# Moving the ordered expert list and one gather ahead of a product, loading gate weights earlier, and packing two weight chunks per buffer slot

## Chip, cores and metric

The kernel runs on one core of one Trainium2 chip. The metric is device time in microseconds (us) of one execution of the program. The inputs are fixed, so every run does the same work.

## What is computed

Three layers follow each other. The first is attention over 4 batches, 12 heads, 448 positions and 64 values a head, in which the heads are mixed by one small matrix before the softmax and by another behind it. The second is a dense layer with an ELU between two matrices. The third sends each of the 1792 rows to one of 8 experts, or to none:

```python
h = x @ w_in                                   # 1792x768 @ 768x2048
x = np.where(h > 0.0, h, np.exp(np.minimum(h, 0.0)) - 1.0) @ w_out
do_compute = x @ w_skip > 0                    # rows that go to an expert at all
logits = x[do_compute] @ w_gate                # 8 logits a row
e_idx = np.argmax(logits, axis=1)
gate_w = softmax(logits)[arange, e_idx]
for e in range(8):                             # rows of expert e alone
    out[e's rows] = x + gate_w * (relu(x @ w1[e]) @ w2[e])
# all other rows: out = x
```

## The kernel before

TensorE (PE) multiplies in fp32r terms: a number is split into a high part (a cast on ScalarE, ACT) and the rest (a subtraction on VectorE, DVE), and each product is three matmuls, high by high, high by low and low by high. So each weight chunk and each tile of activations is cast on ACT and subtracted on DVE before PE can use it.

**First dense product (`products`, L582, PE from about 376 to 608 us).** 16 chunks of `w_in` (`fc`) by 4 batches. Its outputs go through the ELU (`elu`) to DRAM as `gT`. In the same stretch `tables` (L530 on) clears the table of slots, loads the gate matrix `w_gate` and the column `w_skip` into `wgt`, turns `wgt` with six small PE transposes (`pt<-ident,wgt`, L545), and stores the turned rows as `wg` for a later broadcast. Where an instruction is issued from this point on is decided by a scheduler when the program is built (the hand-written order ends at `order.close()`), with `behind(...)` as the one way to hold an instruction back.

**Second dense product (L855, PE from about 608 to 853 us).** 14 tiles of 128 rows; each is 16 chunks `fc` of `w_out`, three terms and two halves of the columns, 96 matmuls in all. The first nine chunks (`EARLY`) are already split when it begins. The other seven are read back from DRAM (`wr<-wf`, L801) into the pool `raw0`, which has three slots (`R0`) of 1536 numbers a partition. A chunk needs 768 of them, and has a slot of its own, so the fourth load waits until DVE has subtracted the first chunk. Behind the last of these loads stand two broadcast loads of the gate rows (`wrow<-wg`, L805, 1920 and 1536 KB), held there by `behind(last_wr)`. The activations of a tile come in four chunks `gr<-gT` (L727), which ACT casts and DVE subtracts to `gh`. All of these loads are issued by SyncE (SP), in its order.

**Routing (`score`, `route`, `seat`).** For each finished tile DVE forms nine dot products with the gate rows (L745), finds the best expert (L751, L753), takes the exponentials on ACT (L758) and their sum's inverse (`sm`, `pairs`), and makes a flag `do` (L764) and a one-hot row `oh` (L766). `seat` counts the rows of each expert with PE (`pp`, L773 and L775), computes the slot of each row, and GpSimd (POOL) scatters row number and gate weight into `slots` in DRAM. For the last two tiles a 128 by 128 matrix `hot` (L787) gathers the rows of expert 0 with PE: `place_old` adds those of older tiles, two matmuls for each of six column blocks `k` (L826, L827), and L900 adds those of the last one. Blocks 0 to 4 stand ahead of the last tile's `seat`, block 5 behind it.

**Experts (PE from 860 us on).** POOL reads the lists of rows back (`ids<-slots`): experts 1, 0 and 2 singly, then experts 3 to 7 in one DMA (L1146, 640 pieces of 8 bytes). `plan` chooses the fullest of experts 3 to 7, which gets a second tile and goes last. `reorder` (L983 on) therefore makes the lists `ordered`: a memset and six small operations on DVE, of which the first (`swapped<-ids`, L987) reads the lists of experts 3 to 7 and the third (`ordered`, L991) completes all but the last expert's. `gather` (L1028) fetches the rows of an expert by an indirect DMA on POOL, and PE transposes them (`turn_x`, L1038).

Weights come in 64 chunks of 768 KB (L1010), 15 slots deep. `use` takes the next chunk and has the one two places ahead split by ACT (`whi`, L1021) and DVE (`wlo`, L1023). `expert_first` is x by w1 (L1050), `expert_second` h by w2 (L1063); h is turned to `ht` (L1038 to L1040) in between. The order around the change:

```python
expert_first([0], [h], ...)
expert_second(0, ht, ...)
expert_first([1], [h], ...)
reorder()
xg[3] = gather(ids[3])
...                       # e = 1: xg[4]; expert_first([2]); expert_second(1), in which xg[3] is turned
```

Of the kernel before, what the change touches and what calls it, by code (L numbers as in the profile page):

```python
# [431 lines left out]
def mixtures(tc, order, xT, w_in, w_out, w_skip, w_gate, w1, w2, ident, gT, wf, wg, x2d, slots, out):  # L432
# [5 lines left out]
    with ExitStack() as top:  # L438
# [27 lines left out]
        with ExitStack() as ctx:  # L466
# [63 lines left out]
            def tables():  # L530
# [7 lines left out]
                nc.sync.dma_start(out=x2d[NT:NT + 1, :], in_=wgs[0:1, :])  # L538
                nc.sync.dma_start(out=wgt[:, :, :E], in_=w_gate.rearrange("(k p) e -> p k e", p=128))
                nc.sync.dma_start(out=wgt[:, :, E], in_=w_skip.rearrange("(k p) -> p k", p=128))  # L540
                nc.sync.dma_start(out=wg[E:E + 1, :], in_=w_skip.unsqueeze(0))
# [125 lines left out]
            elu(1)  # L667
            load_x(3)
            products(2)
            w_jobs(0)  # L670
# [30 lines left out]
        with ExitStack() as ctx:  # L701
# [47 lines left out]
            def route(i, lg):  # L749
                mx = st_p.tile([128, 8], FP32, tag="mx", name="mx")  # L750
                nc.vector.max(out=mx, in_=lg[:, :E])  # L751
                ix = st_p.tile([128, 8], U32, tag="ix", name="ix")
                nc.vector.max_index(out=ix, in_max=mx, in_values=lg[:, :E])  # L753
                nmx = st_p.tile([128, 1], FP32, tag="nmx", name="nmx")
                nc.vector.tensor_scalar(out=nmx, in0=mx[:, 0:1], scalar1=-1.0, scalar2=None, op0=ALU.mult)
# [4 lines left out]
                nc.vector.reciprocal(out=pairs[:, i, 1:2].bitcast(FP32), in_=sm)  # L760
                ef = st_p.tile([128, 1], FP32, tag="ef", name="ef")
                nc.vector.tensor_copy(out=ef, in_=ix[:, 0:1])
                do = st_p.tile([128, 1], FP32, tag="do", name="do")
                nc.vector.tensor_scalar(out=do, in0=lg[:, E:E + 1], scalar1=0.0, scalar2=None, op0=ALU.is_gt)  # L764
                oh = st_p.tile([128, E], FP32, tag="oh", name="oh")
                nc.vector.tensor_scalar(out=oh, in0=iota8, scalar1=ef, scalar2=do, op0=ALU.is_equal, op1=ALU.mult)  # L766
                return i, oh, do
# [30 lines left out]
            gs = {0: load_g(0)}  # L798
            for fc in range(EARLY, NF):
                raw = raw0.tile([128, 2 * DM], FP32, tag="w", name="wr")[:, :DM]  # L800
                last_wr = nc.sync.dma_start(out=raw, in_=wf[fc - EARLY])  # L801
                wo[fc] = split(raw, ring_a if fc < RA + RB else ring2)
            for part in (slice(0, 5), slice(5, E + 1)):
# [40 lines left out]
            for i, n, fc, cs in work:  # L844
# [35 lines left out]
                if fc == NF - 1:  # L880
                    if 0 in cs:
                        x2 = rows[i] = x2_p.tile([128, DM], FP32, tag="x2", name="x2")
                    for c in cs:
                        to, at = x2[:, cols[c]], po[c][:, :cols[c].stop - cols[c].start]
                        nc.scalar.copy(out=to, in_=at)  # L885
                        if last and c == 1:
                            turned, freed = score_turned(x2, c)
                            place_old(range(2))
                            logits(turned)
                            place_old(range(2, 5))  # L890
                    if 1 in cs:
# [3 lines left out]
            hot = seat(*route(NTILE - 1, lg))  # L895
            place_old(range(5, NK))
            xt0 = [gh_p.tile([128, 2, GC, 128], FP32R, tag="gh", name=f"xt0{c}") for c in range(2)]
# [8 lines left out]
        with ExitStack() as ctx:  # L906
# [288 lines left out]
            h, ht = new_h(), []  # L1195
            expert_first([0], [h], jobs(((3, 2), turn_h, h, ht, 0)))
            expert_second(0, ht, jobs(((0,), turn_h, h, ht, 1), ((2,), turn_x, 1)))
            h = new_h()
            expert_first([1], [h], jobs(((1, 2), turn_x, 2)))
            reorder()  # L1200
            xg[3] = gather(ids[3])
            base = nc.values_load(tab[0:1, 3, E:E + 1], engines=(SP,), min_val=0, max_val=E * CAP)
# [108 lines left out]
```

## Time and profile before

| | us |
|---|---|
| Three timed runs | 1047.15, 1040.65, 1037.43 |
| Median of these | 1040.65 |
| The profiled execution's own time | 1035.86 |
| Its span, first to last instruction | 1034.1 |
| DVE, ACT and POOL busy in the span | 768.2, 531.8, 228.3 |

Busy times are averages over stages with different limits. A row of the timeline has start, length, engine, source line, operation, what it writes and reads, and how many were merged; brackets give the idle time of the engine before it and what ended that. SPq is the queue of SP, PEld the weight loads of PE.

### The profile page before, as it was taken

What the parts mean: (1) busy time and instruction counts of PE and PEld (TensorE: products, weight loads), DVE (VectorE), ACT (ScalarE), POOL (GpSimd) and SP (SyncE); (2) the same over time, 40 slices, a digit from 0 to 9 for tenths busy, and PEclk for the clock granted to TensorE, in tenths of its full rate; (3) what the DMA queues carried; (4) which work ended last, traced back from release to release, by engine and by line L of the source; (5) the groups of instructions that cost most, each with busy time, mean ns of one, the idle gap of its engine ahead of it and who ended that gap; (6) DMA issues with size and microseconds to landing.
All of it is one profiled execution on the core that took longest, in us unless ns stands there. A gap on an engine that the chain in (4) does not pass through costs nothing. (4 is left out here: it accounts for less than half of the span.)

```text
span 1034.1 us, 30182 instructions
## 1 busy us (share of the span) xinstructions
PE 993.6 (96%) x12226; PEld 874.0 (85%) x12226; DVE 768.2 (74%) x1589; ACT 531.8 (51%) x1077; POOL 228.3 (22%) x295
## 2 busy tenths in 40 slices
PE   7899999999999899999999999999999999899997
PEld 4577777777777688999999998999999998798987
DVE  6678788788788788767666576868686848999963
ACT  5557567567666565444544453121212107788861
POOL 2134224223322312222333200101000003312001
PEclk9899999999999999999999999999999999999999
DMA  5555566466555685545665469633343387999800
GB/s 166 198 174 145 166 217 181 150 205 192 156 185 179 179 248 190 158 163 173 222 216 194 170 211 311 205 92 123 93 122 96 99 310 264 394 395 399 340 9 34
DMA packets 134219, 199.69 MB, mean 193 GB/s; under 512 B 35860, under 2 KB 101400, under 8 KB 133821
## 3 DMA queue, kind: packets, MB, share of 16 engines
q1 hardware_dynamic: 131933, 191.27, 56.2%
q0 software_dynamic: 2144, 6.46, 1.6%
q8 instruction: 97, 1.59, 0.7%
q14 instruction: 45, 0.37, 0.1%
HBM read 122.47 MB, written 37.65 MB: 155 GB/s over the span
## 5 line engine op out<-in xcount | busy, mean ns | idle before, releaser
L855 PE MATMUL o<-w,gh 128*128 128x384 f32 (+2 forms) x1344 | 238.9, 337 | 2.2 <-ACT w L460 1.6
L855 PEld LDWEIGHTS o<-w,gh 128*128 128x128 f32 x1344 | 231.9, 188 | 5.3 <-ACT w L460 2.0
L582 PE MATMUL h<-xh,w 128*128 128x448 f32 x1152 | 234.5, 365 | 0.0
L582 PEld LDWEIGHTS h<-xh,w 128*128 128x128 f32 x1152 | 216.1, 188 | 17.6 <-issue 0.2
L243 PEld LDWEIGHTS f<-kr,e 64*64 64x64 f32 x5888 | 121.5, 137 | 51.0 <-issue 34.0
L229 POOL TENSOR_SCALAR kr<-kpost,rs 128x60 f32<-128x60 f32 x184 | 80.9, 454 | 252.4 <-DVE rs L225 227.8
L243 PE MATMUL f<-kr,e 64*64 64x60 f32 x5888 | 121.5, 223 | 9.6 <-issue 3.6
L745 DVE SCALAR_TENSOR_TENSOR junk<-x,wrow 128x768 f32<-128x768 f32 x117 | 111.8, 955 | 18.1 <-ACT x L885 12.8
L1023 DVE TENSOR_TENSOR wlo<-w1t,whi 128x1536 fp32r<-128x1536 f32 x64 | 110.9, 1751 | 14.3 <-ACT whi L1021 13.9
L208 DVE TENSOR_REDUCE nmx<-c 128x1 f32<-128x448 f32 x184 | 106.2, 619 | 19.5 <-PE c L200 19.2
L217 ACT ACTIVATE e<-c,nmx 128x448 f32<-128x448 f32 x184 | 114.4, 639 | 2.1 <-DVE nmx L208 2.1
L248 ACT COPY at<-f 128x480 f32<-128x480 f32 (+1 forms) x92 | 52.1, 566 | 114.2 <-PE f L243 114.2
L497 POOL TENSOR_TENSOR wf<-a,p 128x768 f32<-128x768 f32 x32 | 66.6, 2082 | 178.1 <-DVE p L495 141.1
L1021 ACT CAST whi<-w1t 128x1536 fp32r<-128x1536 f32 x64 | 93.9, 1482 | 20.6 <-PE ph L1050 9.9
L200 PE MATMUL c<-d,kpre_up 60*64 60x448 f32 x368 | 94.1, 565 | 1.6 <-ACT s L163 1.6
L264 PEld LDWEIGHTS xp<-at,v 128*64 128x64 f32 (+1 forms) x1536 | 74.0, 135 | 24.7 <-issue 14.1
L264 PE MATMUL xp<-at,v 128*64 128x120 f32 (+3 forms) x1536 | 91.1, 265 | 3.6 <-DVE rs L225 1.8
L200 PE MATMUL c<-d,kpre_low 64*64 64x448 f32 x368 | 91.5, 552 | 2.9 <-DMA d<-s 2.9
L159 PE MATMUL qk<-k,qq 64*120 64x448 f32 (+1 forms) x576 | 80.0, 400 | 8.1 <-ACT k L138 5.1
L730 ACT CAST gh<-gr 128x512 fp32r<-128x512 f32 x56 | 35.0, 625 | 98.7 <-PE o L855 38.8
L159 PEld LDWEIGHTS qk<-k,qq 64*120 64x120 f32 (+1 forms) x576 | 52.6, 182 | 23.5 <-ACT k L138 5.9
L248 DVE COPY at<-f 128x480 f32<-128x480 f32 (+1 forms) x92 | 58.8, 640 | 13.9 <-PE f L243 9.7
(177 smaller groups left out, 1251.8 us busy)
## 6 DMA issues: line engine op xcount, KB each, us to landing
w1t<-in_moe_w_dram SPq DMA_DIRECT2D x64, 768.0 KB
d<-s SPq DMA_DIRECT2D x176, 210.0 KB
gT<-g SPq DMA_DIRECT2D x64, 224.0 KB
f<-in_moe_w_in_dram SPq DMA_DIRECT2D x16, 768.0 KB
f<-in_moe_w_out_dram SPq DMA_DIRECT2D x16, 768.0 KB
gr<-gT SPq DMA_DIRECT2D x48, 256.0 KB
rk<-in_k_dram SPq DMA_DIRECT2D x24, 224.0 KB
xr<-xT SPq DMA_DIRECT2D x24, 224.0 KB
```

The source lines that it names most:

```text
L159: nc.tensor.matmul(out=ps[:n, :S], lhsT=qt[T, p // 2][rows, a, p % 2, :n], rhs=kt[b, p][rows, z, :], start=(i == 0), stop=(i == 2))
L200: nc.tensor.matmul(out=ps[j * UP:(j + 1) * UP, :S], lhsT=kpre_up[UP:UP + HP, :] if z else kpre_low, rhs=d[z, j])
L208: nc.vector.tensor_reduce(out=t, in_=c, op=ALU.max, axis=AX.X, negate=True)
L217: nc.scalar.activation(out=e, in_=c, func=ACTF.Exp, bias=t, accum_out=sms[U][:, i:i + 1])
L243: nc.tensor.matmul(out=ps[to, c // 2, :, z, :], lhsT=e[rows, keys], rhs=kr[rows, :])
L248: copy(out=to[:, :, r + j * m:r + (j + 1) * m], in_=at[:, :, first:first + m])
L264: nc.tensor.matmul(out=ps[z * 64:(z + 1) * 64, i, :n], lhsT=t[:, z, jc % t.shape[2], :], rhs=att[T][:t.shape[0], jc, 2 * p + z, :n], start ...
L582: nc.tensor.matmul(out=ps, lhsT=w[:, a, kk, :], rhs=xs[tb, kk][:, z, :], start=(kk == 0 and a + z == 0), stop=(kk == NK - 1 and a == 1))
L745: nc.vector.scalar_tensor_tensor(out=t[:, o:o + n], in0=x2, scalar=1.0, in1=w, op0=ALU.mult, op1=ALU.mult, accum_out=lg[:, e:e + 1])
L855: mm = nc.tensor.matmul(out=po[c][:, :cols[c].stop - cols[c].start], lhsT=gs[i][fc // GC][:, a, fc % GC, :], rhs=wo[fc][:, z, cols[c]], st ...
L1021: nc.scalar.copy(out=hi, in_=t)
L1023: nc.vector.tensor_tensor(out=lo, in0=t, in1=hi, op=ALU.subtract)
```

## The change

It makes five edits. Three move code: the loads of `wgt` go from `tables` to a place ahead of the third group of `products`; the flag and the one-hot in `route` go ahead of the exponentials; `reorder` and the gather for expert 3 go from behind expert 1's first product to behind expert 0's first product. One packs two chunks of the dense weights into one slot of `raw0`. One moves block 4 of `place_old` behind the last `seat`.

```diff
@@ tables
-                nc.sync.dma_start(out=wgt[:, :, :E], in_=w_gate.rearrange("(k p) e -> p k e", p=128))
-                nc.sync.dma_start(out=wgt[:, :, E], in_=w_skip.rearrange("(k p) -> p k", p=128))
@@
             load_x(3)
+            nc.sync.dma_start(out=wgt[:, :, :E], in_=w_gate.rearrange("(k p) e -> p k e", p=128))
+            nc.sync.dma_start(out=wgt[:, :, E], in_=w_skip.rearrange("(k p) -> p k", p=128))
             products(2)
@@ route
                 nc.vector.max_index(out=ix, in_max=mx, in_values=lg[:, :E])
+                ef = st_p.tile([128, 1], FP32, tag="ef", name="ef")
+                nc.vector.tensor_copy(out=ef, in_=ix[:, 0:1])
+                do = st_p.tile([128, 1], FP32, tag="do", name="do")
+                nc.vector.tensor_scalar(out=do, in0=lg[:, E:E + 1], scalar1=0.0, scalar2=None, op0=ALU.is_gt)
+                oh = st_p.tile([128, E], FP32, tag="oh", name="oh")
+                nc.vector.tensor_scalar(out=oh, in0=iota8, scalar1=ef, scalar2=do, op0=ALU.is_equal, op1=ALU.mult)
                 nmx = st_p.tile([128, 1], FP32, tag="nmx", name="nmx")
...
                 nc.vector.reciprocal(out=pairs[:, i, 1:2].bitcast(FP32), in_=sm)
-                ef = st_p.tile([128, 1], FP32, tag="ef", name="ef")
-                nc.vector.tensor_copy(out=ef, in_=ix[:, 0:1])
-                do = st_p.tile([128, 1], FP32, tag="do", name="do")
-                nc.vector.tensor_scalar(out=do, in0=lg[:, E:E + 1], scalar1=0.0, scalar2=None, op0=ALU.is_gt)
-                oh = st_p.tile([128, E], FP32, tag="oh", name="oh")
-                nc.vector.tensor_scalar(out=oh, in0=iota8, scalar1=ef, scalar2=do, op0=ALU.is_equal, op1=ALU.mult)
@@
-            for fc in range(EARLY, NF):
-                raw = raw0.tile([128, 2 * DM], FP32, tag="w", name="wr")[:, :DM]
-                last_wr = nc.sync.dma_start(out=raw, in_=wf[fc - EARLY])
-                wo[fc] = split(raw, ring_a if fc < RA + RB else ring2)
+            for f0 in range(EARLY, NF, 2):
+                raw = raw0.tile([128, 2, DM], FP32, tag="w", name="wr")
+                fcs = range(f0, min(f0 + 2, NF))
+                for fc in fcs:
+                    last_wr = nc.sync.dma_start(out=raw[:, fc - f0], in_=wf[fc - EARLY])
+                for fc in fcs:
+                    wo[fc] = split(raw[:, fc - f0], ring_a if fc < RA + RB else ring2)
@@ last tile
-                            place_old(range(2, 5))
+                            place_old(range(2, 4))
...
-            place_old(range(5, NK))
+            place_old(range(4, NK))
@@ experts
             expert_first([0], [h], jobs(((3, 2), turn_h, h, ht, 0)))
+            reorder()
+            xg[3] = gather(ids[3])
             expert_second(0, ht, jobs(((0,), turn_h, h, ht, 1), ((2,), turn_x, 1)))
             h = new_h()
             expert_first([1], [h], jobs(((1, 2), turn_x, 2)))
-            reorder()
-            xg[3] = gather(ids[3])
```

What the scheduler makes of it is seen in the order of the instructions. On PE, at the start of the dense layer, the transposes of the gate matrix `wgt` stand among the products `h`; before:

```order
L264 MATMUL xp<-at,v 64x88 x48
L582 MATMUL h<-xh,w 128x448 x175
L545 MATMUL pt<-ident,wgt 8x128 x6
L582 MATMUL h<-xh,w 128x448 x959
L855 MATMUL o_10422<-w,gh 128x384
```

And now:

```order
L264 MATMUL xp<-at,v 64x88 x48
L580 MATMUL h<-xh,w 128x448 x126
L543 MATMUL pt<-ident,wgt 8x128 x6
L580 MATMUL h<-xh,w 128x448 x1008
L858 MATMUL o_10419<-w,gh 128x384
```

The transposes moved 49 matmuls forward.

On SP, at the start of the second dense product, `wr` is a chunk of weights, `gr` one of activations (`gT_0_61`, `65`, `69` and `73` are the four of tile 1, those ahead of them tile 0's), `gT` a store of the first product, `wrow` the gate rows; before:

```order
L801 DMA wr<-wf_79 128x768
L727 DMA gr<-gT_0_61 128x4x128
L727 DMA gr<-gT_0_65 128x4x128
L593 DMA gT_3_76<-g 128x448
L727 DMA gr<-gT_0_69 128x4x128
L801 DMA wr<-wf_80 128x768
L727 DMA gr<-gT_0_73 128x4x128
L727 DMA gr<-gT_0_61 128x4x128
L801 DMA wr<-wf_81 128x768
L801 DMA wr<-wf_82 128x768
L801 DMA wr<-wf_83 128x768
L805 DMA wrow<-wg 128x3840
```

And now:

```order
L803 DMA wr<-wf_80 128x768
L591 DMA gT_3_76<-g 128x448
L803 DMA wr<-wf_81 128x768
L803 DMA wr<-wf_82 128x768
L727 DMA gr<-gT_0_61 128x4x128
L727 DMA gr<-gT_0_65 128x4x128
L803 DMA wr<-wf_83 128x768
L808 DMA wrow<-wg 128x3840
L808 DMA wrow<-wg 128x3072
L727 DMA gr<-gT_0_69 128x4x128
L727 DMA gr<-gT_0_73 128x4x128
L895 DMA x2d<-x_10517 128x768
```

Chunks 13 and 14 (`wf_81`, `wf_82`) moved ahead of all of tile 1's activations, and the last two of those (`69`, `73`) moved behind both loads of the gate rows.

On DVE, during expert 0's two products, `wlo` is a weight chunk's low part, `ht` that of the turned hidden tile, and the short operations belong to `plan`; before:

```order
L932 CAST pair<-ix 128x1
L951 TENSOR_SCALAR ni<-ni 1x8
L1023 TENSOR_TENSOR wlo<-w1t,whi 128x1536
L934 TENSOR_SCALAR pbase<-pair 128x1
L953 TENSOR_SCALAR ov<-ni 1x8
L1040 TENSOR_TENSOR ht_13081<-pt_13082,ht_13081 128x512
L936 TENSOR_SCALAR star<-ebase,pbase 128x8
```

And now:

```order
L935 CAST pair<-ix 128x1
L954 TENSOR_SCALAR ni<-ni 1x8
L990 TENSOR_TENSOR swapped<-ids 128x8
L937 TENSOR_SCALAR pbase<-pair 128x1
L956 TENSOR_SCALAR ov<-ni 1x8
L1026 TENSOR_TENSOR wlo<-w1t,whi 128x1536
L939 TENSOR_SCALAR star<-ebase,pbase 128x8
L948 TENSOR_SCALAR tab<-pbase 1x1
L1043 TENSOR_TENSOR ht_13078<-pt_13079,ht_13078 128x512
```

The first operation of `reorder` now stands ahead of a `wlo` and of the first `ht`; `ordered` is the seventh short operation behind that `ht`. Before, the first operation of `reorder` stood 41 rows behind `ni`. On POOL the gathers for experts 3 and 4 moved ahead of expert 0's scatter of results.

## Rows read from the trace of the kernel before

**Rows 1.** The page, busy time of the engines: us, share of the span, instructions.
```profile
PE 993.6 (96%) x12226; PEld 874.0 (85%) x12226; DVE 768.2 (74%) x1589; ACT 531.8 (51%) x1077; POOL 228.3 (22%) x295
```

**Rows 2.** PE's waits, whole span: us in total, times, longest.
```profile
PE pt L1038 <- DMA xg<-x2d,ordered: 3.0, 1, 3.0
...
PE o L855 <- ACT w L460: 1.6, 1, 1.6
...
PE pt L545 <- DMA wgt<-in_moe_w_gate_dram: 1.3, 1, 1.3
...
PE o L855 <- DVE w L461: 0.6, 2, 0.4
...
PE pp L773 <- DVE ps L779: 0.3, 1, 0.3
```

**Rows 3.** PE timeline, start of the first dense product and the gate's transposes.
```profile
376.06 36.41 PE L582 MATMUL h<-xh,w 128*128 128x448 f32 x175
413.81 0.82 PE L545 MATMUL pt<-ident,wgt 128*8 128x128 f32 x6 [1.34 <-DMA wgt<-in_moe_w_gate_dram]
```

**Rows 4.** SP timeline, loads of activations and of the gate weights.
```profile
382.35 2.77 SPq L508 DMA_DIRECT2D xr<-xT  x6
...
410.40 0.40 SPq L539 DMA_DIRECT2D wgt<-in_moe_w_gate_dram  x1
```

**Rows 5.** PE timeline, start of the second dense product.
```profile
608.36 13.77 PE L855 MATMUL o<-w,gh 128*128 128x384 f32 x78
```

**Rows 6.** SP timeline, second dense product: last chunk loads, gate rows, activations.
```profile
617.50 2.65 SPq L801 DMA_DIRECT2D wr<-wf  x3
620.24 0.94 SPq L805 DMA_DIRECT2D wrow<-wg  x2
...
629.92 4.32 SPq L727 DMA_DIRECT2D gr<-gT  x3
```

**Rows 7.** ACT timeline, same stretch: cast of chunk 13, cast of an activation chunk.
```profile
622.88 0.83 ACT L460 CAST w<-wr 128x768 fp32r<-128x768 f32 x1 [2.85 <-DMA wr<-wf]
...
637.10 0.62 ACT L730 CAST gh<-gr 128x512 fp32r<-128x512 f32 x1 [8.04 <-DMA gr<-gT]
```

**Rows 8.** DVE timeline, experts 0 to 2.
```profile
868.96 0.15 DVE L951 TENSOR_SCALAR ni<-ni 1x8 int32<-1x8 int32 x1
...
871.08 0.67 DVE L1040 TENSOR_TENSOR ht<-pt,ht 128x512 fp32r<-128x512 f32 x1
...
892.67 0.15 DVE L991 TENSOR_TENSOR ordered<-ids,swapped 128x8 int32<-128x8 int32 x1
```

**Rows 9.** Stretch, length, busy PE, PEld, DVE, ACT, POOL (count), granted clock, DMA share, GB/s.
```profile
624.00:632.00 8.00, 7.40 (x41) 6.72 (x41) 5.06 (x7) 2.96 (x5) 0.00 (x0) 1.00 1.01 427
```

**Rows 10.** DVE timeline, second dense product: first dot product of tile 0.
```profile
630.13 0.96 DVE L745 SCALAR_TENSOR_TENSOR junk<-x,wrow 128x768 f32<-128x768 f32 x1 [2.81 <-DMA wrow<-wg]
```

**Rows 11.** PE timeline, experts 0 and 1.
```profile
871.93 1.55 PE L1063 MATMUL y<-whi,ht 128*128 128x384 f32 x8
...
901.31 0.30 PE L1038 MATMUL pt<-ident,xg 128*128 128x128 f32 x1 [2.97 <-DMA xg<-x2d,ordered]
```

**Rows 12.** DMAs of line 1028 between 880 and 905, gathers: issue to landing.
```profile
DMA to landing us min/median/max: 6.9/7.3/8.1
```

**Rows 13.** Columns as in rows 9, two stretches of the experts.
```profile
860.00:880.00 20.00, 19.75 (x108) 17.71 (x107) 19.21 (x35) 16.82 (x18) 7.10 (x8) 1.00 0.79 270
880.00:900.00 20.00, 18.34 (x89) 15.11 (x87) 19.79 (x39) 15.21 (x17) 8.69 (x4) 1.00 1.04 395
```

**Rows 14.** POOL timeline: the issue of the lists of experts 3 to 7.
```profile
863.93 0.91 POOL L1146 DMA_DIRECT2D ids<-slots  x1
```

**Rows 15.** DMA of line 1146, those lists: us from issue to landing.
```profile
DMA to landing us min/median/max: 5.6/5.6/5.6
```

**Rows 16.** DVE timeline, the last tile's routing.
```profile
856.76 0.15 DVE L759 TENSOR_SCALAR sm<-sm 128x1 f32<-128x1 f32 x1 [0.36 <-ACT ex L758]
```

**Rows 17.** PEld timeline, weights of the last tile's gather by matrix.
```profile
859.03 1.42 PEld L900 LDWEIGHTS pt<-hot,x 128*128 128x128 f32 x12 [0.29 <-DVE hot L787]
```

## The prediction

> **What bounds the kernel now.** First I read the busy times: PE works 993.6 of the span's 1034.1 us, the next engine 768.2 [rows 1]. So what can be gained on PE is small beside the whole, and the view to read next is PE's list of waits. The reader is to look there for waits that the edited lines can reach, and finds four: 3.0 us for the gather of expert 3, 1.6 and 0.6 us for the cast and the subtraction of a dense chunk, 1.3 us for the gate weights, and 0.3 us in the last tile's seat [rows 2]. They add up to 6.8 us, 0.7% of the execution. Third, I went to each of these places in the timelines, to see what would be late next once the wait is gone.
>
> **Part 1, gate weights loaded sooner.** PE's transposes stand behind 175 products that took 36.41 us, 0.208 us each, and wait 1.34 us; the load was issued at 410.40, 3.4 us before they start at 413.81 [rows 3, 4]. Now they stand behind 126 products, so PE reaches them at 376.06 + 126 x 0.208 = 402.3 us. The loads are issued right behind the last six activation loads, at about 385.1 [rows 4], 17 us earlier than needed. On SP two issues, the first of 0.40 us [rows 4], together about 0.8, go ahead of the load of the next `w_in` chunk; PE works without a gap there [rows 3], and I count that as hidden by it. Without that cover it would be the 0.8 us. Value: -1.3, bounds -1.3 and 0.
>
> **Part 2, two chunks in a slot.** PE did the 78 matmuls of tile 0's first 13 chunks in 13.77 us, 0.1766 us each, and then stood still for chunk 13 [rows 5]. The last three chunk loads were issued from 617.50 on, because each waited for a slot; the first was ready for ACT at 622.88, 5.4 us on [rows 6, 7]. Now chunks 13 and 14 need no such wait: they are issued as soon as the last two stores of `gT` let SP pass, some 4 to 5 us earlier. Chunk 15 waits for the subtraction of the first two, as the load at 617.50 did. DVE now does that ahead of two activation chunks instead of behind them, and a subtraction of 128 x 512 takes 0.67 us [rows 8]. So I put its issue near 616; by the same 5.4 us it is there by 621.4, and PE needs it at 608.36 + 90 x 0.1766 = 624.3. So all of 1.6 + 0.6 = 2.2 us goes.
>
> What comes late next is tile 1's last two activation chunks, which now stand behind both gate-row loads. PE reaches tile 1 at 608.36 + 96 x 0.1766 = 625.3, its third chunk at 633.8, that chunk's low part at 634.5. The gate rows are 3456 KB, 8.3 us at the 427 GB/s that the trace shows while they move [rows 9]; from 621.4 on they are through at 629.7, and two loads of 256 KB more at about 631. DVE first does six dot products of tile 0, 0.96 us each and a short read behind each [rows 10], say 626.4 to 632.6, and then this low part, done near 633.3. That leaves 1.2 us of slack, little. If instead the chunk is no earlier than the activation chunk behind the gate rows was before, ACT starts on it at 637.10, needs 0.62 us [rows 7], DVE 0.67 more, and PE has stood from 634.5 to 638.4: 3.9 us. Value: -2.2, bounds -2.2 and +1.7. I take the first, since the loads ahead of it now start earlier by four to five us.
>
> Here the Trainium skill has a rule that speaks against the change: "DMA: Bandwidth & Descriptors", section "Queues, rings and completion order", says that each DMA engine takes the descriptors of one issuer's ring in order. By that the two activation loads cannot overtake the gate rows, and the trace agrees: the one behind them was issued at 629.92 and cast at 637.10, after 8.04 us in which ACT had nothing else to do [rows 6, 7].
>
> **Part 3, the list and the gather.** PE waits 2.97 us at 901.31 for expert 3's rows [rows 11]. The list they need was complete at 892.67 on DVE [rows 8], and a gather lands 6.9 to 8.1 us after its issue [rows 12]. Now the list is made among the operations around 872, so the gather is issued near 874 and lands near 882, 16 us before PE turns the rows. The 3.0 us goes.
>
> It is not free. DVE's queue is full here, 19.21 and 19.79 of 20 us [rows 13], and `swapped<-ids`, now right behind the operation at 868.96 [rows 8], waits for a DMA. That DMA was issued at 863.93 and landed 5.6 us later, at 869.5 [rows 14, 15]. Behind the waiting instruction stand a weight subtraction and the first `ht`, which ended at 871.75 [rows 8]; PE takes that `ht` in the matmuls from 871.93 on [rows 11], a slack of 0.2. DVE is held from 869.0 to about 869.6, and up to three short operations of 0.15 us now come ahead of that `ht`; before, DVE waited about 0.2 us there for ACT. So `ht` comes some 0.6 us later and PE about 0.4 to 0.5 us. The other five operations only change their places, so DVE's sum stays; I add 0.1 for one more low part late by that. Cost +0.6, net -2.4. Bounds: -3.0, if the list is there in time, and 0, if it lands 8.1 us after issue, as the latest gather does: 872.0, 3.0 us late, with no cover on DVE.
>
> For the list itself the Trainium skill has a price: the same page, "Anatomy of one DMA", fits a DMA issued from GpSimd by about 2.0 us and the bytes at 436 GB/s. By that 5 KB would land at 866, nothing would wait, and the sum would be better by the 0.5 us. The row has 5.6 us for 640 pieces of 8 bytes, and the sum goes by the row.
>
> The third and fourth gathers also come ahead of expert 0's scatter in POOL's queue; results of expert 0 are read by nobody, and POOL is busy 7.10 and 8.69 of 20 us [rows 13]. That is hidden by all the later work; without it the scatter would end a microsecond or two later.
>
> **Part 4, flag and one-hot first, one block later.** In the last seat DVE idles 0.36 us for ACT's exponentials ahead of `sm` and the one-hot [rows 16], and PE's weight load for `hot` waits 0.29 us [rows 17]. The one-hot no longer waits, and PE asks for the count two pairs of matmuls earlier, but the pairs are only put behind it. Value -0.1; bounds -0.6 (both waits) and +0.3.
>
> **Sum.** -1.3 - 2.2 - 2.4 - 0.1 = -6.0 us. From the profiled execution's 1035.86 (span 1034.1 and 1.8 around it) that makes 1029.9. The timed runs have their median 4.8 us higher, at 1040.65, and span 9.7 us; taken off that median, the forecast is 1034.6. A difference of 1% (10.4 us) is about what a measurement of this kernel can tell from none; this is 0.6%. PE's granted clock is 1.00, the 2.4 GHz level, in all stretches read [rows 9, 13], the one with PE's stand of 3.0 us too, so I expect nothing from it.
>
> **The rivals.**
> - *DVE takes the gather's gain.* For it: 39.0 of 40 us busy up to 900. PE's stand of 3.0 us gave DVE time; without it low parts would come late one after another. Against it: ACT and DVE wait for PE again soon after. If only 0.5 of the 3.0 us is left, the sum is -1.3 - 2.2 - 0.5 - 0.1 = -4.1: 1036.5.
> - *Tile 1's chunk comes at its old time.* For it: the ring order above. Then part 2 is +1.7, the sum -2.1: 1038.5.
> - *The list does not hold DVE* and the seat's waits go: -1.3 - 2.2 - 3.0 - 0.6 = -7.1: 1033.5.
> - *Slower: the list falls behind weight loads.* SP issues 768 KB loads at the same time. Each takes 2.0 us at 395 GB/s [rows 13]. From a landing 7 us or more after 869.0, that is over 12 us after issue, the wait eats the other -6.6. Behind seven loads it would land at 863.93 + 7 x 2.0 = 877.9, hold DVE 8.9 us and PE about 8.7: +2.1, 1042.8. Against it: 5.6 us measured with the same loads in flight.
> - *A move doesn't do what it says*, for instance the gather still late: +2.4 on the forecast, 1037.0. The order of instructions speaks against it.
>
> **How the numbers follow.** Forecast 0.52, DVE 0.2, tile 1 0.1, nothing held 0.1, slower 0.04, no effect 0.04. All of them lie within 1% of 1040.65; only the scatter of the timed runs, 9.7 us over three, can carry a median past 10.4. So faster by over 1% gets 0.12, slower 0.04, within 1% 0.84. The range, from the far case below less the scatter of a median to the tile 1 case with some of it above: 1029.0 to 1040.0.
>
> **What would show it.** In PE's list of waits the rows for the gather, for `w` and for `wgt` should be gone. In DVE's timeline `swapped<-ids` should stand near 869 with a wait of half a microsecond, and PE should show a short wait for `ht`. A PE wait for `gh` some 25 us into the second dense product would be the tile 1 case, several for `wlo` between 875 and 900 the DVE case. The forecast is wrong if the PE waits go and the span shrinks by less than 4 us, or by more than 8.

## The result and the profile after

| | us |
|---|---|
| Changed kernel, median of 10 runs | 1030.45 (1028.40 to 1036.95) |
| Kernel before, median of 10 runs beside it | 1041.03 (1037.43 to 1048.04) |
| Ratio | 0.9898, 95% interval 0.9867 to 0.9929 |
| Profiled execution and its span, after | 1029.92, 1028.1 |

The gain is 10.6 us, 1.0%, with an interval from 7.4 to 13.8 us. The forecast was 1034.6, a gain of 6.0 us: the time lies inside the range, the gain is larger than its sum, and it sits on the border between "within 1%" and "faster". The span of the two profiled executions fell by just the 6.0 us forecast, from 1034.1 to 1028.1; the sections below show why that pair agrees by luck. The prediction named a span that shrinks by more than 8 us as a sign that it is wrong: the spans of this pair don't give that sign, but the medians are 10.6 us apart. The ratios in this document leave out executions that lie far above the others of their kernel, among them one of 1924.3 us of `p1_gate`.

PE's list of waits of the changed kernel, which answers to [rows 2]:

```profile
PE qk L159 <- ACT k L138: 5.0, 2, 4.6
PE f L243 <- issue: 3.4, 4, 1.3
...
PE lg L834 <- ACT tx L844: 0.5, 1, 0.5
PE pp L773 <- DVE ps L779: 0.3, 1, 0.3
PE pt L1041 <- ACT h L1059: 0.3, 1, 0.3
```

The waits for the gather, for `w` and for `wgt` are gone, and no row for `gh` or `wlo` has come. What is left in the edited stretches is 0.5, 0.3 and 0.3 us. One of these, `pp` behind `ps`, is the seat's 0.3 us that the prediction counted among its places: it stayed. The long rows belong to attention, which the change doesn't touch.

PE's timeline of the two dense products after, to be read beside [rows 3, 5]:

```profile
376.79 25.71 PE L580 MATMUL h<-xh,w 128*128 128x448 f32 x126
402.33 0.82 PE L543 MATMUL pt<-ident,wgt 128*8 128x128 f32 x6
402.91 204.29 PE L580 MATMUL h<-xh,w 128*128 128x448 f32 x1008
607.03 33.24 PE L858 MATMUL o<-w,gh 128*128 128x384 f32 x190
```

The transposes stand behind 126 products (one product here is one matmul `h`) without idle time, at the 402.3 that was forecast. The second dense product runs through its first 190 matmuls without a gap; before, it stopped after 78.

SP, ACT and DVE in that stretch, which answer to [rows 6, 7]:

```profile
611.07 0.93 SPq L803 DMA_DIRECT2D wr<-wf  x2
...
615.86 0.33 SPq L803 DMA_DIRECT2D wr<-wf  x1
616.29 0.86 SPq L808 DMA_DIRECT2D wrow<-wg  x2
617.20 3.12 SPq L727 DMA_DIRECT2D gr<-gT  x2
...
620.06 0.83 ACT L460 CAST w<-wr 128x768 fp32r<-128x768 f32 x1 [0.74 <-DMA wr<-wf]
...
630.26 1.35 ACT L730 CAST gh<-gr 128x512 fp32r<-128x512 f32 x2 [5.62 <-DMA gr<-gT]
...
631.00 1.34 DVE L731 TENSOR_TENSOR gh<-gr,gh 128x512 fp32r<-128x512 f32 x2
```

Chunk 15 was issued at 615.86 ("near 616") and cast at 620.06. Tile 1's late chunks stand behind the gate rows, as feared; their casts begin at 630.26 after 5.62 us, their low parts end at 632.34. PE's first tile takes 96 x 0.175 us, so tile 1 begins at 623.8 and needs the third chunk's low part 9.2 us later (634.5 less 625.3 in the prediction), at 633.0. That low part is the first of the two, done at about 631.7. The slack is 1.3 us by this count, and 1.1 by the trace, where the matmul that reads it starts at 632.8; 1.2 was forecast. So this rival did not come about.

The list and the gather, on POOL, then on DVE and PE, to be read beside [rows 8, 11, 14]:

```profile
859.30 0.90 POOL L1149 DMA_DIRECT2D ids<-slots  x1
...
869.52 0.95 POOL L1031 DMA_INDIRECT xg<-x2d,ordered  x1 [3.12 <-DVE swapped L995]
...
865.64 0.15 DVE L990 TENSOR_TENSOR swapped<-ids 128x8 int32<-128x8 int32 x1
...
866.18 1.76 DVE L1026 TENSOR_TENSOR wlo<-w1t,whi 128x1536 fp32r<-128x1536 f32 x1 [0.26 <-issue]
...
868.06 0.67 DVE L1043 TENSOR_TENSOR ht<-pt,ht 128x512 fp32r<-128x512 f32 x1
...
898.73 0.82 PE L1041 MATMUL pt<-ident,xg 128*128 128x128 f32 x6
```

`swapped` did not wait for the list, which landed 4.8 us after its issue. The gather went out at 869.52 and PE took its rows at 898.73 without a wait. But `ht` is late all the same: the first 16 matmuls `y` take 3.29 us instead of 2.88. And one thing was not foreseen at all, in the stretches of the seat (columns as in [rows 9]):

```profile
850.00:852.00 2.00, 1.66 (x12) 1.48 (x13) 1.41 (x16) 1.68 (x4) 0.01 (x1) 1.00 1.05 406
852.00:854.00 2.00, 2.00 (x15) 2.00 (x15) 1.01 (x8) 0.22 (x2) 1.01 (x1) 0.72 0.33 128
854.00:856.00 2.00, 2.00 (x12) 2.00 (x11) 0.24 (x3) 0.00 (x0) 0.78 (x1) 0.50 0.00 0
856.00:858.00 2.00, 2.00 (x13) 1.77 (x13) 0.81 (x2) 1.25 (x3) 0.58 (x2) 0.92 0.01 0
```

The granted clock falls to 0.50, the 1.2 GHz level, for some 3.4 us, behind PE's two short stands of 0.5 and 0.3 us. The trace of before has the same two stands, at 854.64 and 855.74, and 1.00 behind them:

```profile
856.00:858.00 2.00, 1.93 (x18) 1.84 (x18) 1.18 (x11) 0.60 (x3) 1.01 (x1) 1.00 0.84 333
858.00:860.00 2.00, 1.90 (x17) 1.71 (x16) 0.74 (x5) 0.00 (x0) 0.14 (x1) 1.00 0.04 13
```

### The profile page after: what moved, and what is told of

Read it like the earlier page. It is cut to its first block, busy times and chain, and to the rows that moved or that the text cites. A ratio compares the mean times of both kernels' runs of the same rounds, so it can differ in the third digit from the quotient of the medians.

```text
span 1028.1 us, 30177 instructions
## 1 busy us (share of the span) xinstructions
PE 993.9 (97%) x12226; PEld 874.4 (85%) x12226; DVE 766.1 (75%) x1589; ACT 532.1 (52%) x1077; POOL 247.2 (24%) x295
## 5 line engine op out<-in xcount | busy, mean ns | idle before, releaser
L243 PEld LDWEIGHTS f<-kr,e 64*64 64x64 f32 x5888 | 118.7, 135 | 51.8 <-issue 35.4
```

Of the source, the lines that this page charges most:

```text
L243: nc.tensor.matmul(out=ps[to, c // 2, :, z, :], lhsT=e[rows, keys], rhs=kr[rows, :])
```

## The experiments

Two theories were put against each other first. T1: a PE wait costs its listed idle time and a fixed piece more, in which PE starts again. T2: the list is the price, and the rest is scatter. A third question is whether part 4 brings the dip of the clock (Da) or chance does (Db). Since a median over ten runs moves by some us by itself, the theories are judged by stretches of PE's work, taken from the starts of the same matmuls in each trace: `h0` is the start of the first product `h` (all of attention lies before it but its last 6 us, which stand behind the first 18 products), A runs from there to the first `o`, B to the 251st `o`, C to the last, D to the first expert matmul `ph`, E from there to the last `y`. An asterisk marks a dip of the clock in the stretch (for E behind the gather's place, for D at the seat, for A at the transposes). The A of p3_list holds one more, at its very start (370.8), behind a stand of 2.3 us at the end of attention. The A of stops and stands is left out, since their added work lies in it.

```
               h0      A        B      C       D      E
before         365.97  242.39   47.10  197.53  7.54   166.41
before_again   363.42  242.67   47.48  197.54  8.80*  167.74*
p1_gate        369.86  243.42   45.15  197.53  9.11*  167.83*
p2_pack        368.54  246.60   44.01  197.26  7.53   166.36
p3_list        370.75  248.11   46.29  197.54  9.06*  163.63
p4_seat        365.24  244.43*  47.69  197.53  8.79*  167.98*
after          366.69  240.34   44.01  197.26  8.79*  163.75
after_again    366.20  240.81   44.01  197.26  8.79*  163.73
list_job       365.47  240.68   44.01  197.26  7.16   163.46
list_job_b     364.82  240.81   44.01  197.25  7.17   163.38
seat_fill      370.48  240.80   44.01  197.26  6.22   163.39
seat_fill_b    367.21  241.27   44.01  197.26  6.21   164.95
stops          365.91  -        44.01  197.26  8.79*  163.38
stands         367.34  -        44.01  197.26  7.16   164.81
```

### The four parts alone

Each is the kernel before with one hunk of the change: `p1_gate` the loads of `wgt` ahead of `products(2)`, `p2_pack` the packed slots, `p3_list` the list and the gather, `p4_seat` the flag, the one-hot and block 4.

```diff
+            nc.sync.dma_start(out=wgt[:, :, :E], in_=w_gate.rearrange("(k p) e -> p k e", p=128))
+            nc.sync.dma_start(out=wgt[:, :, E], in_=w_skip.rearrange("(k p) -> p k", p=128))
             products(2)
```

> Part 1 alone: the gate weights are loaded ahead of the third group of products, nothing else changes. Two theories of what a removed PE wait is worth. T1, list plus restart: the idle time in the list of waits (1.34 us) and about 0.25 us more, in which PE fills again. T2, the list alone, and what the trace showed beyond it is scatter of other stages. T1: in the trace, from PE's first product h at 376 to the first matmul of the second dense product, PE needs 1.6 us less than before (232.3 us there). T2: 1.3 us less. Both: the wait for wgt is gone from PE's list, the waits for the chunk w (1.6 us) and for the gather (3.0 us) stay. A third possibility, that the rate of the products ahead of the transposes (0.2067 us each before, 0.2027 after) belongs to this part: then another 0.6 to 0.8 us goes. The time itself, with its scatter of some us, will not be told from before.

```diff
-                raw = raw0.tile([128, 2 * DM], FP32, tag="w", name="wr")[:, :DM]
+                raw = raw0.tile([128, 2, DM], FP32, tag="w", name="wr")
```

> Part 2 alone: two dense chunks per slot. T1 (list plus restart, three restarts at about 0.25 us): from the first matmul of the second dense product to the last one of tile 1, PE needs 3.0 us less than before. T2 (the list alone): 2.0 to 2.2 us less. Both: no PE wait for w is left, and none for gh of tile 1. If the restart of the products is what was saved instead, the difference stands elsewhere.

```diff
+            reorder()
+            xg[3] = gather(ids[3])
             expert_second(0, ht, jobs(((0,), turn_h, h, ht, 1), ((2,), turn_x, 1)))
```

> Part 3 alone: the ordered list and the gather for expert 3 behind expert 0's first product. The PE wait for the gather (3.0 us) goes. T1: from the first expert matmul to the last, PE needs 3.2 - 0.4 = 2.8 us less than before; T2: 3.0 - 0.4 = 2.6 us less. Theory H (as predicted): the first operation of the list waits on DVE for the read of the lists, some 0.5 us, and PE gets the first ht 0.4 to 0.5 us late. Theory S: the list is there in time, and the three short operations now ahead of the low part and of ht make the delay, about 0.4 us all the same. Here, without the clock's dip that the changed kernel showed at the seat, the list has no 1.3 us of extra time, so H would show an idle time of DVE ahead of that operation that ends with the DMA, S none.

```diff
-                            place_old(range(2, 5))
+                            place_old(range(2, 4))
```

> Part 4 alone: flag and one-hot ahead of the exponentials, block 4 behind the last seat. Da, the clock's dip (1.2 GHz for 3.4 us from 852.9 on, in the changed kernel) comes from this part: it shows here too, within 850 to 862, and PE needs 1.3 us more from the last o matmul to the first expert matmul. Db, the dip falls by chance: not here, or no more often than elsewhere. Without a dip this part is worth 0 to -0.3 us between these two places, since PE's wait for the counts (pp behind ps, 0.3 us) stays.

Measured, as ratios to before: 0.9962 (0.9926 to 0.9997), 0.9942 (0.9913 to 0.9972), 0.9981 (0.9943 to 1.0018) and 0.9990 (0.9953 to 1.0028). They add up to -1.25%, as much as the whole change (-1.02%) within their intervals. So no part is seen to give back what another gains; but only the first two are clear of no effect, and the intervals are too wide to show that the parts are independent.

Stretch B settles T1 against T2 for the chunks: 44.01 in every trace with part 2, and in the traces without it more than that by 3.09, 3.47, 1.14, 2.28 and 3.68 us (before, before_again, p1, p3, p4), where the lists of waits name 2.2, 2.3, 0.55, 1.1 and 2.3 us in 3, 4, 2, 3 and 5 stands. Each stand cost 0.28 to 0.39 us more than listed (0.39 in p3_list, which has one more stand at 632.6, too short for the list). So T1 in its amount. What the fixed piece is made of can be read from the single matmuls of these traces. The list counts from the end of the last matmul `o`, which the profile models 0.338 us behind its start, while in the running stream the next one starts after 0.174: that makes 0.16 us. The second matmul behind a stand starts 0.28 us after the first: 0.11 us more. So the larger piece is in how the list counts, and only the smaller one is a slower start of PE. In p1_gate, where only the subtraction is waited for, the rows are these:

```profile
613.28 14.12 PE L855 MATMUL o<-w,gh 128*128 128x384 f32 x80
627.66 2.38 PE L855 MATMUL o<-w,gh 128*128 128x384 f32 x12 [0.27 <-DVE w L461]
630.32 9.86 PE L855 MATMUL o<-w,gh 128*128 128x384 f32 x55 [0.28 <-DVE w L461]
```

At the gather 2.97 listed cost 3.20 (from the last `ph` of expert 1's first product to the 64th `y`, 15.17 before and 11.97 after), and at the transposes 0.16 us went on top, in all five traces. In A, however, T1 and T2 can't be told apart, and p1_gate missed both: its A should have been 1.6 or 1.3 us shorter than before's, and is 1.0 longer. The step of the products, the time from one start to the next, shows why. Two other traces, p2_pack and then before_again (seen from 376 us on):

```profile
416.48 0.82 PE L545 MATMUL pt<-ident,wgt 128*8 128x128 f32 x6 [2.21 <-DMA wgt<-in_moe_w_gate_dram]
417.06 198.25 PE L582 MATMUL h<-xh,w 128*128 128x448 f32 x959
```

```profile
375.67 34.25 PE L582 MATMUL h<-xh,w 128*128 128x448 f32 x165
411.41 0.82 PE L545 MATMUL pt<-ident,wgt 128*8 128x128 f32 x6 [1.49 <-DMA wgt<-in_moe_w_gate_dram]
411.99 194.27 PE L582 MATMUL h<-xh,w 128*128 128x448 f32 x959
```

The same 959 products take 198.25 us in one trace and 194.27 in the other, 0.207 or 0.203 us each, at a granted clock of 1.00. Ahead of the transposes before_again went at 0.208, behind them fast; p2_pack and p3_list the other way round. And where PE was slow it came later and waited less: 1.34 and 1.49 us in the two traces of before, 2.1 to 2.2 in the three others. The trace that the forecast was made from had the smallest of five waits. In p1_gate the products went slow at 502, behind two starts 0.34 and 0.32 us apart, and stayed so to the end. It and seat_fill_b also stood 0.37 and 0.54 us near 400 for the low part of an activation (`xh`), a wait that no other trace lists.

For part 4, stretch D of these traces has two levels: 7.53 and 7.54 without the dip, 8.8 to 9.1 with it, and the dip is there with part 4 and without it. Da falls. For part 3, `swapped` in p3_list waited for the list, 0.16 us, in spite of a dip at the seat, and `y` took 3.19 over its first 16.

### Both kernels again, the list one job later, and the seat

The first two are the changed kernel and the kernel before without an edit.

> The changed kernel once more. Across the six traces so far four things differ by chance: the end of attention (the first product h starts between 365.2 and 370.7), dips of the granted clock to 0.5 for 3.4 us (1.3 to 1.6 us each), the step of the products h (0.200 or 0.207 us each, with a change of step at the gate's transposes in three of the four traces that wait for wgt there), and the seat. If the dip at the seat falls by chance (it was there in four of six, with part 4 in two of three and without it in two of three), it may or may not be here. If the step of h changes only where PE stood, no change of step is here at the transposes. What must repeat if my reading is right: 44.0 us from the first o matmul to the 251st, 163.7 us from the first to the last expert matmul, y 3.2 to 3.3 us over its first 16.

> The kernel before once more. T1 and the four traces that hold the wait for wgt or for w: 1.3 to 2.2 us listed at wgt, 1.1 to 3.7 us lost at the chunks w between the 78th and the 96th o matmul, 2.8 to 3.0 us at the gather. If waits bring dips of the clock behind them, a dip within 4 us behind the gather's wait (two of four so far) or behind the one for wgt (one of four). A step of h that changes at the transposes would be the fourth of five.

`list_job` makes the list one job later:

```diff
-            reorder()
-            xg[3] = gather(ids[3])
-            expert_second(0, ht, jobs(((0,), turn_h, h, ht, 1), ((2,), turn_x, 1)))
+            expert_second(0, ht, jobs(((0,), turn_h, h, ht, 1), ((1,), early_list), ((2,), turn_x, 1)))
```

> The changed kernel with the list and the gather put one job later, behind the second weight chunk of expert 0's second product, so that the first ht no longer stands behind the list's operations; the gather is issued some 4 us later, at about 874, still 20 us ahead of its use. If the short operations and the wait for the read of the lists are what delays the first ht: y's first 16 matmuls take 2.9 us (3.29 in the changed kernel, 2.88 before), and first to last expert matmul takes 163.3 us instead of 163.7. If the delay comes from something else in the change, it stays at 3.2 to 3.3. The wait for the gather stays gone in either case. The time itself moves by less than a measurement tells.

`seat_fill` is list_job with the matmuls of `place_old` in another order (block 1 and 2 held behind the last transposes of `x`):

```diff
-                            place_old(range(2))
+                            place_xp((0, 3))
+                            with behind(turn_mm[0]):
+                                place_xp((1, 2))
                             logits(turned)
-                            place_old(range(2, 4))
+                            place_xp((4,))
+                            place_hot((0, 1, 2))
```

> list_job, and PE's small matmuls of the last tile in another order, so that they stand in its two waits there: the transposes of block 1 and 2 behind those of the last tile's x, all the others of the old rows ahead of the counts. Computes the same. If PE's two listed waits in the seat (lg behind tx 0.46 and pp behind ps 0.27) can be covered: from the last o matmul to the first expert matmul 0.7 us less without a dip (7.54 before, of which 7.53 was seen again), by T1 up to 1.1 less. Rival: DVE's chain from the logits to hot sets this stretch, PE then waits for hot instead, and it is 0 to 0.4 less. If the dip at the seat comes from PE's two stands there, there is none now; if it falls by chance, it may still be there, with 1.3 us. Beside the changed kernel: 1 to 1.5 us less in all, too little for the medians, to be read from the stretches.

after_again: 1031.4, ratio 0.9900 (0.9868 to 0.9933); B, E and `y` (3.30) repeat to 0.02 us. Not so the step: it changed at the transposes, where PE had not stood, and twice more by 418. before_again: 1.49 us listed at `wgt`, 3.47 lost at the chunks, 2.97 at the gather, and there the clock fell while PE stood:

```profile
898.00:900.00 2.00, 0.00 (x0) 0.00 (x0) 1.80 (x3) 2.00 (x2) 0.00 (x0) 1.00 1.08 417
900.00:902.00 2.00, 1.30 (x5) 1.33 (x6) 2.00 (x2) 0.40 (x1) 0.00 (x0) 0.53 1.00 383
902.00:904.00 2.00, 2.00 (x9) 2.00 (x8) 0.52 (x2) 1.47 (x1) 0.00 (x0) 0.62 1.03 385
```

PE does nothing from 898 to 900 and then works at half the clock. This happened in three of the five traces with the gather's wait and in none of the nine without it; it costs 1.3 to 1.6 us of E. At the seat the dip came in 7 of the 12 traces that have both stands there (4 of 7 with part 4, 3 of 5 without), at the transposes in 1 of 5 with a stand and in none without.

list_job: `y` back at 2.94, E 163.46, the wait for the gather still gone; 1026.9, ratio 0.9857 (0.9822 to 0.9892). On DVE:

```profile
863.36 1.76 DVE L1026 TENSOR_TENSOR wlo<-w1t,whi 128x1536 fp32r<-128x1536 f32 x1 [0.16 <-ACT whi L1024]
...
865.17 0.67 DVE L1043 TENSOR_TENSOR ht<-pt,ht 128x512 fp32r<-128x512 f32 x1
...
868.61 0.15 DVE L990 TENSOR_TENSOR swapped<-ids 128x8 int32<-128x8 int32 x1
```

The order of before is back around `ht`, so the delay came with the list's place. D is 7.16, which is part 4's own worth without a dip: 0.4 us. seat_fill: D 6.22 and 6.21, 0.9 less than list_job and twice without a dip, so the two stands could be covered. PE then stood 0.30 us for `hot`, as the rival on record has it, and D fell all the same by more than the lists say (0.73 less 0.30); 1031.1, ratio 0.9895 (0.9855 to 0.9936).

### Repeats, and a price for stands that was missed

> list_job once more, beside seat_fill on the same chip, for a comparison of the two with the changed kernel (1030.45 and 1031.4 us in two sets). Its first trace had no dip at the seat and 163.46 us from the first to the last expert matmul against 163.73 and 163.75. So it should be 0.3 us faster than the changed kernel, which no median shows; a median as low as its first one (1026.9) would be scatter of attention and dips in its favour and should go back to 1029 to 1031. Repeats if right: y's first 16 in 2.9 us.

> seat_fill once more. Its first trace: 6.22 us from the last o matmul to the first expert matmul, no dip, against 7.16 in list_job without a dip and 8.8 in the changed kernel with one. If its stand-free seat keeps the dip away, 6.2 again; if the dip falls by chance there too, about 7.5. In the medians it should be 1 us faster than list_job and, where the dip at the seat is kept away (six of eight traces without this edit had it or not by chance: five with, three without among those with PE's two stands), another 0.8 on average; together less than the scatter of attention.

(That text counts the dips wrongly: nine traces had both stands by then, six with a dip and three without.) list_job_b: 1031.8, ratio 0.9907 (0.9874 to 0.9941), so the first median was scatter; E 163.38 and `y` 2.92 repeat. seat_fill_b: 1028.6, ratio 0.9867 (0.9839 to 0.9895). Neither is shown to beat the changed kernel. In seat_fill_b what the seat gained was lost again, as PE and POOL show:

```profile
873.79 0.85 PE L1052 MATMUL pt<-ident,xg 128*128 128x128 f32 x6 [1.36 <-DMA xg<-x2d,ids]
...
864.78 2.60 POOL L1042 DMA_INDIRECT xg<-x2d,ids  x1 [3.32 <-DMA ids<-slots]
```

PE comes to the experts sooner, POOL doesn't: its gather waits for its list, and PE stands 1.36 us for the rows, at a place where no other trace has a wait. The early seat alone didn't make it, since seat_fill was as early and PE didn't stand: this list landed 5.6 us after its issue, where the eleven other traces that record it have 2.0 or 2.1.

`stops` and `stands` add nine more loads of the gate matrix with their transposes, whose results are read by nobody; in `stands` each load is held behind a product:

```diff
+                with behind(last_mm[0]):
+                    nc.sync.dma_start(out=g2[:, :, :E], in_=w_gate.rearrange("(k p) e -> p k e", p=128))
...
+                        nc.tensor.transpose(pt[:E, i * 128:(i + 1) * 128], g2[:, c * 3 + i, :E], ident)
```

> The changed kernel with nine extra loads of the gate matrix in the first dense product, each turned by six small PE transposes like the real one, so that PE stands nine more times for such a load; what they make is read by nobody. It measures the disputed price of a stand. T1, refined by the traces of the kernel before and of the parts alone, where the products lost 2.08, 2.24, 2.94, 2.87 and 2.95 us at the transposes with 1.34, 1.49, 2.21, 2.13 and 2.22 us listed as idle, and 0.58 without a stand: the loss is 0.58 + the listed idle + 0.16, at each of the nine. T2: 0.58 + the listed idle. On the step of the products h (0.200 or 0.207 us): if a stand draws it anew, it changes at some of the nine, as it did at four of the five stands so far; if a stand has nothing to do with it, it changes no more often than between them. On the clock: one dip (0.5 for 3.4 us) in five such stands so far, so one to three in nine if a stand brings them on, none if they fall by chance as between stands.

> The kernel of the run stops did not make PE stand: the nine extra loads came early enough, and each set of transposes cost 0.57 or 0.58 and 0.09 us. Here each of the nine loads is held until PE has done the twelfth of the 18 products ahead of its transposes, so that PE reaches these some 1.2 us after the load is issued and must stand for it. Price of a stand: T1, the gap between the last product ahead and the first behind is 0.58 + the listed idle + 0.16 (0.28 by the two stands for DVE g in stops, 0.50 and 0.77 us listed); T2, 0.58 + the listed idle. Step of the products: if stands draw it anew, it is slow (0.207 us) behind some of the nine and fast (0.200) behind others, and changes at the stands and not between; in stops it stayed fast through all nine sets of transposes without a stand, and was slow for 24 products behind a stand of 0.50. If the step does not hang on stands, it stays fast here too. Clock: one dip in five stands for wgt so far; if stands bring dips on, one to three here, in the 4 us behind a stand; if not, none.

Both missed their aim: the loads were there in time in all 18 places, PE never stood for one, and each set of transposes cost 0.67 us (1036.17 and 1037.12 us, one execution each). What they show is by the way. PE stood for the ELU twice in each; of stops:

```profile
470.77 3.97 PE L580 MATMUL h<-xh,w 128*128 128x448 f32 x18 [0.50 <-DVE g L590]
474.58 0.82 PE L701 MATMUL pt<-ident,g 128*8 128x128 f32 x6
475.15 22.06 PE L580 MATMUL h<-xh,w 128*128 128x448 f32 x108
```

0.50 and 0.77 us listed cost 0.78 and 1.05, T1 once more with 0.28. Behind the first stand the step is slow up to the next transposes, behind the second it stays fast. And `stands` has the changed kernel's order of the list without a dip at the seat, which none of the other traces has. PE, POOL and DVE there:

```profile
863.68 1.64 PE L1071 MATMUL ph<-whi,xt 128*128 128x512 f32 x6
...
867.81 0.90 POOL L1167 DMA_DIRECT2D ids<-slots  x1
...
873.63 0.17 DVE L1008 TENSOR_TENSOR swapped<-ids 128x8 int32<-128x8 int32 x1 [1.38 <-DMA ids<-slots]
...
876.44 1.66 PE L1084 MATMUL y<-whi,ht 128*128 128x384 f32 x8 [1.24 <-DVE ht L1061]
```

The list is issued 4.1 us after the first `ph` and lands 5.8 us later. DVE wants it 8.5 us after the first `ph`, and is held 1.38 us; PE stands 1.24 us for `ht`. With the dip PE and DVE come 1.6 us later (D is 8.79 against 7.16) and POOL does not: in the changed kernel the list was issued 2.2 us after the first `ph` and was there at 7.0. So the dip hid the hold that was forecast.

## Why the prediction was right, and which steps were mis-sized

The path was right in the main: the waits for the gather, for `w` and for `wgt` went (the seat's 0.3 us for `ps` stayed), tile 1's chunk came in time, `ht` came 0.1 to 0.4 us late where 0.4 to 0.5 was priced (1.5 in stands, without the dip), and all gains are on PE. Against the table, the sum is too small because three terms are. By the means of the table, with the thing and without it:

| Step | Forecast | Measured |
|---|---|---|
| Part 1, gate weights | -1.3 | A: -3.7 (244.8 in five traces with the wait, 241.2 in seven without) |
| Part 2, chunks | -2.2 | B: -2.7 (46.7 in five, 44.0); C: -0.3 |
| Part 3, list and gather | -2.4 | E: -3.4 (167.3 in five, 163.9 in the five with the changed order) |
| Part 4, seat | -0.1 | D: -0.3 (8.4 in five, 8.1 in seven with the two stands) |

Together -10.4, where the medians differ by 10.6; of these, 1.7 us in A, what goes beyond the stand itself, are not shown to be the change's (below). `h0`, which the change doesn't touch, lies between 363.4 and 370.8 and makes up much of the scatter of the runs. That the spans of the first two traces differ by just 6.0 is luck: before had the shortest wait for `wgt` of five traces and no dip at the seat or the gather, after had a dip at the seat. The second pair's spans, 1035.0 and 1028.5, are 6.5 apart, but there `h0` lies 2.8 us earlier in the kernel before; from `h0` on, the pairs differ by 6.7 and 9.3.

*Part 1.* The step that failed is "Value: -1.3", the listed wait of one execution. The stand itself was worth 1.5 to 2.4 us in five traces, 2.0 on average, by its length and 0.16 us that the list leaves out. The rest of the 3.7 is the step of the products behind it (slow to the end in two of the five traces with the stand, 4.0 us each; in one of the seven without it, from about 500 on) and a dip of the clock in two of the five, of which one lies ahead of the stand and has nothing to do with it. That the stand sets the step is not shown: both go together, but the step also changed where PE did not stand, and the two runs meant to test it made no stands.

*Part 2.* The listed 2.2 left out the fixed piece of each stand, 0.3 us three times. Tile 1's late chunks behaved as worked out, with 1.1 us of slack for 1.2; the rule on one issuer's ring in the Trainium skill, "DMA: Bandwidth & Descriptors", section "Queues, rings and completion order", held again (5.62 us of wait behind the gate rows) and cost nothing. The 0.3 in C is the wait of `tx` for ACT, listed 0.3 in all traces without part 2 and in none with it; the forecast did not name it, and why it went was not tried. In the list of before it is this row:

```profile
PE tx L840 <- ACT x L885: 0.3, 1, 0.3
```

*Part 3.* The 3.0 us of the gather went, with 0.2 more, and with them a dip in three cases of five. The hold on DVE, forecast at 0.6 with a wait of `swapped` for the list, is 0 to 1.4: 0 in the changed kernel, where the sign named for it didn't show, 0.2 in p3_list, both with a dip at the seat, and 1.4 in stands without one, all within the bounds given. Even without a wait for the list, `y` lost 0.4 in both traces of the changed kernel, behind a DVE idle of 0.26 that no record explains, and 0.1 in stops. list_job takes all of it away.

*Part 4.* Worth 0.4 without a dip, more than the 0.1 taken and within its bounds.

*The clock.* "I expect nothing from it" was wrong as such, and not only in size. It rested on one trace, which happened to have none of the dips at the edited places. The Trainium skill, "TensorE: Matmul & The Clock Gate", section "HAM oscillation — how this bites in real kernels", says that waits for DMA between groups of matmuls bring the clock down. Three of five traces agree at the gather's 3 us stand.

*The rivals.* DVE did not take the gather's gain (E is 2.7 less where neither trace has a dip there), tile 1's chunk was in time, and the list landed 4.8 to 6.5 us after its issue, so it did not fall behind the weight loads.

## What to carry to other kernels

A PE wait was worth more here than the list says: 0.2 to 0.3 us more for each stand, and at the gather, in three traces of five, a dip of the clock too. Take the length of a wait from several traces, since one may hold the shortest, and compare the stretches between the same matmuls: B and C repeat to hundredths where the whole time scatters by ten. Put a small job that waits for a DMA behind the operation that PE needs next on that engine, not ahead of it: the later place cost nothing here, and a wait that one trace hides, the next one shows.

## What the runs showed of the hardware

The products `h` go at one of two mean steps, 0.203 or 0.207 us, at a granted clock of 1.00, and keep it for up to 198 us; over a stage of 1152 that is worth 4 us and more. (The 0.200 of some expectations is found only in short pieces of the faster stream.) What chooses the step stays open. The Trainium skill, "TensorE: Matmul & The Clock Gate", section "Wait — 56ns, not 53.3ns?", gives the columns at 2.4 GHz and 2.5 ns between two starts, by which 448 columns would be an estimate of 189 ns; both measured steps are above it. The products `o` have one step: stretch C repeats to 0.01 us in all fourteen traces once part 2 is told apart.

The clock fell within the gather's stand of 3 us in one trace, behind it in two, and behind the seat's two stands of 0.5 and 0.3 us in seven, for about 3.4 us each time, and the same kernel showed it in one execution and not in another. At the gather it fell in three of five traces with the stand and in none of nine without; at the seat in seven of twelve with the stands and in none of two without, which is too few to show that the stands bring it on.
